# Weights decoded by shift, multiply-add and join, k transposed over the tile of P and sent by DMA, and another order of the program

## The chip, the cores and the metric

The kernel runs on one core of one Trainium2 chip. The metric is the device time of one execution in microseconds (us). The time of the kernel before is the median of three runs.

## What is computed

Gated linear attention followed by a feed-forward layer with ELU, all in float32. The shapes are 4 batches, 8 heads, 768 steps, head size 48; d_model 384, d_ff 2048, so 3072 tokens.

```python
for t in range(S):
    state = alpha[:, :, t, :, None] * state + einsum('bhd,bhe->bhde', k[:, :, t], v[:, :, t])
    y[:, :, t] = einsum('bhd,bhde->bhe', q[:, :, t], state)
x = y.transpose(0, 2, 1, 3).reshape(B * S, H * D)
h = x @ w_in
g = where(h > 0, h, exp(minimum(h, 0)) - 1)
out = g @ w_out
```

q, k, v and alpha are float32. The two weight matrices come in as float64: the kernel gets each value as two 32-bit words and makes a float32 of it on the chip.

## The kernel before

**Two phases that are interleaved.** The attention is cut into 24 windows of 128 steps (six for each batch). The feed-forward layer is cut into 12 blocks of 256 tokens (two windows each) and 8 slices j of d_ff. Weights and activations of the feed-forward layer are split into a high and a low part (type fp32r), and three products replace one: high by high, high by low, low by high.

**The order is written out by hand.** The function body defines small steps, each under a short name. Two strings list them: START for windows 0 to 11 and the first feed-forward blocks, with the decoding of the weights, and STEADY, which is repeated with a shift of two windows and one block a round. A step `KA.4` is step KA of window 4; `A.1.3` is step A of block 1, slice 3; in STEADY the numbers are relative to the round (`A.-2` is the slice two before the block's first one, `U.2` the window two after the round's first). Every engine takes its instructions in the order of the list, and each of its own steps waits for what it needs. DMAs are issued on SP's queue, in the list's order as well.

**The steps of a window i.**
- L (or LA and LB for windows 0 and 1) loads k, q and alpha of the window into one of 3 tiles `qka`; LV loads v into one of 4 tiles `vs`.
- SC: VectorE's running product of alpha, giving P (2 buffers). LN and EX (ScalarE): R = 1/P (2 buffers). KA, KB, KC: k divided by P with one correction step; `d["kt"]` is overwritten. KA and KB are on VectorE for a few windows and on GpSimd for the rest, KC is on VectorE. SQ: q times P into `st` (VectorE or GpSimd). PC: ScalarE copies P into R, for a sum that is checked.
- TP and KN (windows 0 to 5): TensorE transposes k into PSUM, ScalarE copies it to `kn`. TA and TB (windows 6 to 11) and T with a part number (from 12): VectorE transposes k into `kn` by 16 instructions for a window, each of 32 partitions x 128 elements (line 276, `blocks`).
- S: scores, k by q (lines 330 and 314), MK: the mask, on VectorE. U: the state's increments, transposed k by v (lines 376 and 358). UA, UB, UC: the states at the half and the end of the window. UP does part of it on TensorE for window 1.
- Y (for windows 0 to 3 with YL and Y3): the output, state and scores by v. XH, XL: its high and low part into `xt`; XP is XL's subtraction done on TensorE for windows 0 and 1. XD: two DMAs that put the fourth group of heads in its place.

**The steps of the weights.** F loads a weight slice f (768 KB) into `raw`; slices are decoded in pairs p of two slices. DA, DB, DC (lines 565, 571, 577) make the float32 bits from the two words on VectorE. WH (ScalarE) gives the high part, WL (ScalarE for slices 0 and 2, there with WP on TensorE; VectorE for 4; GpSimd for the others) the low part. Slices 2j belong to w_in, 2j + 1 to w_out. LC, CA and CB load a half slice again (`ck`, one buffer) and sum up two checks of its range on ScalarE; V and VP turn all sums into a flag that decides at the end whether a general, slower program must run.

**The steps of a block b and slice j.** A: 18 matmuls of 128x256 (line 639). RA and RB (ScalarE), RC (VectorE): ELU. GH (ScalarE) and GL (VectorE): its high and low part. O: 12 matmuls of 128x384 that add into the output (line 690). Z: two copies and two DMAs of the output.

**The start.** TensorE runs 16 matmuls on constants (X, line 126) until the first window's k is there.

## Time and profile before

| | |
|---|---|
| median of 3 runs | 503.76 us (503.52 to 504.37) |
| the profiled execution's own time | 503.54 us |
| its span, first to last instruction | 501.8 us |
| granted TensorE clock | 1.000 |
| PE (TensorE's matmuls) | 491.7 us busy, 98% of the span |
| PEld (TensorE's weight loads, beside the matmuls) | 474.4 us, 95% |
| DVE (VectorE) | 385.9 us, 77% |
| ACT (ScalarE) | 289.7 us, 58% |
| POOL (GpSimd) | 128.3 us, 26% |
| DMA | 61.13 MB in 22403 packets |

Busy shares are means over the whole span; the slices of the profile show them in 40 equal parts, as tenths. The chain of work follows the execution back from its last instruction, at each step to what released it. Matmuls overlap, so the pace of a group is read from one start to the next and not from the duration of one matmul. A time in square brackets is how long the engine had been idle, with what ended it. SPq is the queue on which SP issues DMAs.

### The profile page before, as it was taken

Reading aid. Unit: us, or ns where it says so; the run is one execution under the profiler, and the core shown is the slowest. Engines: PE = TensorE matmul, PEld = TensorE weight load, DVE = VectorE, ACT = ScalarE, POOL = GpSimd, SP = SyncE. Lnnn points to the kernel's source line nnn. Section 1 sums busy time; section 2 is a strip of 40 time slices with the busy share of each in tenths; the row PEclk is TensorE's granted clock in tenths of the full one; section 3 lists DMA queues with packets and bytes.
Section 4 is the critical chain, followed back from the end, with each engine's and each line's share of the span. In section 5 each row is a group of like instructions: output and inputs, shape, how many; then the busy total and the mean of one; then the engine's idle time right before and its main releaser. Section 6 shows DMA issues by size and latency. Waiting matters only on the chain.

```text
span 501.8 us, 13252 instructions
## 1 busy us (share of the span) xinstructions
PE 491.7 (98%) x5404; PEld 474.4 (95%) x5404; DVE 385.9 (77%) x807; ACT 289.7 (58%) x689; POOL 128.3 (26%) x109
## 2 busy tenths in 40 slices
PE   7999999999999999999999999999999999999996
PEld 3799999999999899999999999999999999999995
DVE  6989999989998579769969969769969878344321
ACT  3656786456460677746755756647755755454432
POOL 4125565443320302501501501501501500000000
PEclk9999999999999999999999999999999999999999
DMA  8999323213522145226245145235233321110001
GB/s 312 413 410 377 97 96 142 88 50 106 189 64 64 51 137 177 65 81 217 55 122 179 48 125 180 58 112 183 72 111 100 92 77 49 51 44 6 3 33 36
DMA packets 22403, 61.13 MB, mean 122 GB/s; under 512 B 2880, under 2 KB 9792, under 8 KB 22336
## 3 DMA queue, kind: packets, MB, share of 16 engines
q1 hardware_dynamic: 22048, 59.83, 36.3%
q8 instruction: 44, 0.72, 0.6%
q10 hardware_dynamic: 288, 0.39, 0.2%
q14 instruction: 23, 0.19, 0.1%
HBM read 53.53 MB, written 4.72 MB: 116 GB/s over the span
## 4 chain that ended last, share of the span: by engine, by line
PE 95%; DVE 2%; ACT 1%; issue 1%; ACTq 0%
PE h L639 40%; PE o L690 40%; PE y L442 4%; PE y L437 2%; PE q L314 2%; PE q L358 1%; PE u L376 1%; PE wp L126 1%; PE sc L330 1%; PE y L481 1%; PE tp L266 1%; DVE kn L276 0%; PE yl L437 0%; PE wd L612 0%; DVE st L342 0%
## 5 line engine op out<-in xcount | busy, mean ns | idle before, releaser
L639 PE MATMUL h<-xt,w 128*128 128x256 f32 x1728 | 215.3, 282 | 0.0
L639 PEld LDWEIGHTS h<-xt,w 128*128 128x128 f32 x1728 | 209.3, 188 | 2.3 <-issue 0.9
L690 PE MATMUL o<-w,gh 128*128 128x384 f32 x768 | 199.3, 341 | 0.8 <-ACT gh L663 0.8
L690 PEld LDWEIGHTS o<-w,gh 128*128 128x128 f32 x768 | 136.8, 188 | 1.7 <-ACT gh L663 1.0
L690 PE MATMUL o<-w,gl 128*128 128x384 f32 x384 | 130.0, 339 | 0.1
L663 ACT CAST gh<-h 128x512 fp32r<-128x512 f32 x96 | 56.0, 583 | 78.4 <-PE o L690 39.9
L676 DVE TENSOR_TENSOR gl<-h,gh 128x512 fp32r<-128x512 f32 x96 | 65.6, 687 | 35.6 <-ACT gh L663 34.4
L276 DVE STREAM_TRANSPOSE kn<-qka 32x128 f32<-32x128 f32 x288 | 87.1, 302 | 4.5
L647 ACT ACTIVATE r<-h 128x512 f32<-128x512 f32 x96 | 57.1, 596 | 47.7 <-PE h L639 39.7
L657 DVE SCALAR_TENSOR_TENSOR h<-r,h 128x512 f32<-128x512 f32 x96 | 64.6, 689 | 17.0 <-ACT r L652 16.2
L690 PEld LDWEIGHTS o<-w,gl 128*128 128x128 f32 x384 | 72.1, 188 | 0.4 <-DVE gl L676 0.4
L222 POOL TENSOR_TENSOR qka<-qka,R 128x512 f32<-128x512 f32 x19 | 26.2, 1378 | 163.9 <-DVE gl L676 116.4
L652 ACT ACTIVATE r<-r 128x512 f32<-128x512 f32 x96 | 59.4, 631 | 0.7
L252 POOL TENSOR_TENSOR st<-qka,P 64x512 f32<-64x512 f32 x36 | 42.8, 1190 | 21.7 <-DVE P L200 16.3
L342 DVE TENSOR_TENSOR st<-q,mask 64x256 f32<-64x256 f32 x72 | 30.4, 422 | 11.8 <-ACT vs L393 9.0
L200 DVE TENSOR_TENSOR_SCAN P<-qka,first 128x516 f32<-128x516 f32 x24 | 30.4, 1267 | 2.8 <-DMA qka<-in_qka_dram 2.3
L227 POOL TENSOR_TENSOR R<-P,R 128x512 f32<-128x512 f32 x20 | 24.2, 1211 | 27.2 <-DVE qka L222 25.8
L209 ACT ACTIVATE R<-P 128x512 f32<-128x512 f32 x24 | 15.2, 632 | 27.7 <-DVE P L200 27.7
L395 DVE TENSOR_TENSOR vs<-vs,q 48x192 f32<-48x192 f32 x30 | 10.5, 349 | 18.0 <-PE q L314 16.1
L495 ACT ACTIVATE y<-y 128x128 fp32r<-128x128 f32 x20 | 5.5, 276 | 29.7 <-PE y L442 26.4
L623 POOL TENSOR_TENSOR w<-spare,w 128x768 fp32r<-128x768 f32 x7 | 15.2, 2173 | 25.8 <-ACT w L603 25.8
L595 ACT ACTIVATE ck<-ck,lim 128x384 f32<-128x384 f32 x32 | 20.7, 646 | 0.1
(100 smaller groups left out, 421.6 us busy)
## 6 DMA issues: line engine op xcount, KB each, us to landing
qka<-in_qka_dram SPq DMA_DIRECT2D x22, 770.0 KB, 6.4
raw<-in_wgt_dram SPq DMA_DIRECT2D x16, 768.0 KB, 13.4
ck<-in_wgt_dram SPq DMA_DIRECT2D x32, 384.0 KB, 3.2
vs<-in_vv_dram SPq DMA_DIRECT2D x36, 192.0 KB, 4.3
out_dram<-ot SPq DMA_DIRECT2D x22, 192.0 KB, 1.9
vs<-in_vv_dram SPq DMA_DIRECT2D x6, 384.0 KB, 12.3
xt<-y SPq DMA_DIRECT2D x40, 48.0 KB, 2.3
qka<-in_qka_dram SPq DMA_DIRECT2D x2, 512.0 KB, 4.9
```

Source lines behind the costliest of these rows:

```text
L200: nc.vector.tensor_tensor_scan(out=P.rearrange("p n w -> p (n w)"), data0=t[:, 2 * NP * W:], data1=first.rearrange("p n w -> p (n w)"), in ...
L222: eng(KAV, i).tensor_tensor(out=d["kt"], in0=d["kt"], in1=d["R"], op=ALU.mult)
L252: eng(SQV, i).tensor_tensor(out=st[r, a], in0=d["q"][r], in1=pw(i)[r], op=ALU.mult)
L276: nc.vector.transpose(out=kn[32 * t:32 * t + 32, :, 32 * g:32 * g + 32], in_=d["kt"][32 * g:32 * g + 32, :, 32 * t:32 * t + 32])
L342: nc.vector.tensor_tensor(out=d["st"][r, a, :, c * C:(c + 1) * C], in0=d["s4"][a][o], in1=mask[o].unsqueeze(1).broadcast_to([64, NP, C]), ...
L639: nc.tensor.matmul(h[:, f, :], lhsT=t[:, wi, ws], rhs=x[:, c, xi, :], start=(f == 0 and k == 0), stop=(k == 8), skip_group_check=True)
L647: nc.scalar.activation(out=r, in_=d["h"], func=AF.Relu, scale=-1.0)
L652: nc.scalar.activation(out=d["r"], in_=d["r"], func=AF.Exp, scale=-1.0)
L657: nc.vector.scalar_tensor_tensor(out=d["h"], in0=d["r"], scalar=-1.0, in1=d["h"], op0=ALU.add, op1=ALU.max)
L663: nc.scalar.copy(out=gh, in_=d["h"])
L676: nc.vector.tensor_tensor(out=gl, in0=d["h"], in1=d["gh"].bitcast(F32), op=ALU.subtract)
L690: nc.tensor.matmul(o[:, 0:DM], lhsT=gt[:, f, ms], rhs=t[:, wi, f * DM:f * DM + DM], start=(j == 0 and f == 0 and k == 0), stop=(j == NJ - ...
```

## The change

**Decoding.** The raw bytes are loaded 5 bytes further into their tile, so that the bits of interest stand in aligned words. DA is a shift of one word, DB a multiply-add over the top byte of each value (type uint8) that writes a small integer into the other word, DC a shift of that word joined with DA's result. The range check becomes narrower: CB makes two passes where it made one, and V compares one more row.

**k for U.** T is now one transposition of 128 x 512 elements that writes into the tile R (which held 1/P and then PC's copy of P). TM is new: four DMAs on SP's queue that bring the pieces to a tile `kx`, 64 KB each in runs of 256 bytes. U reads its stationary operand from `kx` with a step of two elements. TA, TB and `blocks` are gone. TP and KN for windows 0 to 5 stay.

**Order.** START and STEADY are written anew. The first loads, for one, go from LA.0 LB.0 LA.1 LB.1 LV.0 F.2 F.0 L.2 LV.1 to LA.0 LA.1 LB.0 LV.1 LB.1 LV.0 L.2 F.2 F.0.

```diff
 START = """
-LA.0 LB.0 SC.0 LN.0 EX.0 LA.1 KA.0 KB.0 LB.1 SC.1 X.2 LV.0 LN.1 X.2 KC.0 F.2 SQ.0 EX.1 F.0 TP.0 KN.0 S.0 U.0
-SQ.1 UA.0 KA.1 KB.1 MK.0 L.2 KC.1 UC.0 YL.0 LV.1 TP.1 PC.0 Y3.0 Y.0 KN.1 DA.0 PC.1 LV.2 DB.0 L.3 F.4 S.1 SC.2
...
+X.2 LA.0 LA.1 LB.0 SC.0 LN.0 EX.0 LV.1 SQ.0 SC.1 LB.1 X.2 LV.0 KA.0 KB.0 KC.0 SQ.1 TP.0 UB.1 L.2 LN.1 F.2 EX.1 KN.0
+KA.1 S.0 U.0 PC.0 KB.1 MK.0 UA.0 F.0 L.3 KC.1 YL.0 UC.0 TP.1 S.1 KN.1 U.1 SC.2 MK.1 LN.2 DA.0 UB.0 DB.0 F.6 UP.1 Y3.0
+UC.1 UA.1 DC.0 LV.2 F.4 PC.1 YL.1 EX.2 Y3.1 SC.3 KA.2 Y.0 WH.0 Y.1 LN.3 XH.0 F.3 SQ.2 WP.0 EX.3 XH.1 WH.2 WP.2 KA.3
+XP.0 KB.2 WL.0 XP.1 KC.2 TP.2 KB.3 DA.2 S.2 KN.2 XL.0 KC.3 U.2 DB.2 SQ.3 XL.1 F.1 L.4 DC.2 LV.3 TP.3 KN.3 WH.6 DA.1
+A.0.0 UB.2 U.3 UA.2 WH.4 MK.2 UC.2 YL.2 PC.2 WL.4 RA.0.0 F.7 DB.1 RB.0.0 SC.4 DC.1 WL.2 S.3 LN.4 F.5 MK.3 UB.3 WL.6
+A.0.3 WH.3 EX.4 LV.4 DA.3 F.8 SQ.4 A.0.2 UA.3 RA.0.3 Y3.2 A.0.1 YL.3 RC.0.0 RB.0.3 Y.2 KA.4 F.11 DB.3 L.6 KB.4 Y3.3
...
 STEADY = """
-A.-3 Y.1 XH.1 Y.0 XH.0 A.-2 XL.1 RA.-3 O.-5 RA.-2 XL.0 LV.4 U.2 CA.-12 V.0 RB.-3 S.2 UA.2 MK.2.0 U.3 UB.2 S.3
...
+A.-3 CA.-12 Y.1 Y.0 S.2 RA.-3 RB.-3 XH.1 U.2 XH.0 O.-5 L.5 CB.-12 XL.1 RC.-3 UA.2 GH.-3 A.-1 RA.-1 XD.1 XL.0 UB.2
+LC.-11 UC.2 RB.-1 U.3 MK.2.0 S.3 MK.2.1 XD.0 SC.4 LN.4 CA.-11 A.-2 UA.3 EX.4 A.3 RA.-2 UB.3 O.-4 RC.-1 MK.3.0 V.0
+GL.-3 RB.-2 LV.4 RC.-2 KA.4 UC.3 CB.-11 SQ.4 KB.4 MK.3.1 RA.3 LC.-10 A.1 GH.-2 A.0 RA.1 RB.3 RB.1 CA.-10 SC.5 GL.-2
+A.2 GH.-1 RC.1 GL.-1 O.-3 O.-2 LN.5 RA.0 EX.5 L.6 CB.-10 KA.5 KC.4 KB.5 LC.-9 O.-1 RB.0 RC.3 RA.2 RC.0 A.4 PC.4 RB.2
+GH.0 LV.5 GH.1 SQ.5 CA.-9 GL.0 GL.1 RA.4 O.0 CB.-9 RC.2 ZV.4 GH.2 T.4 TM.4 O.1 GL.2 RB.4 KC.5 LC.-8 PC.5 O.2 RC.4
+GH.3 GH.4 GL.4 Z.-1 T.5 VP.0 GL.3 TM.5
...
-    def blocks(i, gs):
...
-        for g in gs:
-            for t in range(4):
-                nc.vector.transpose(out=kn[32 * t:32 * t + 32, :, 32 * g:32 * g + 32],
-                                    in_=d["kt"][32 * g:32 * g + 32, :, 32 * t:32 * t + 32])
...
+    def T(i):
+        d = win[i]
+        tk = d["tk"] = d["R"].rearrange("p n w -> p (n w)").rearrange("p (t b x c) -> p t b x c", t=4, b=2, c=2)
+        nc.vector.transpose(out=tk.rearrange("p t b x c -> p (t b) c x"),
+                            in_=d["kt"].rearrange("p n (j t) -> p t n j", t=4))
+
+    @tok
+    def TM(i):
+        d = win[i]
+        kn = d["kx"] = work.tile([128, 2, 2, 64, 2], F32, name="kn", tag="kn")
+        for g in range(4):
+            nc.sync.dma_start(out=kn[:, :, g // 2, g % 2 * 32:g % 2 * 32 + 32].rearrange("p b x c -> p b (x c)"),
+                              in_=d["tk"][32 * g:32 * g + 32].rearrange("p t b x c -> p (t b) (x c)"))
...
-                nc.tensor.matmul(d["u"][x][64 * a:64 * a + D, n, :], lhsT=d["kn"][r, n, a, 0:D],
+                nc.tensor.matmul(d["u"][x][64 * a:64 * a + D, n, :], lhsT=d["kx"][r, n // 2, a, 0:D, n % 2] if "kx" in d else d["kn"][r, n, a, 0:D],
...
-            raw[p] = wtile(p, [128, 2, WCH, 2], I32, "raw")
-        nc.sync.dma_start(out=raw[p][:, k].rearrange("p k two -> p (k two)"), in_=wgt[f].bitcast(I32))
+            raw[p] = wtile(p, [128, 2, 8 * WCH + 64], U8, "raw")
+        nc.sync.dma_start(out=raw[p][:, k, 5:5 + 8 * WCH], in_=wgt[f].bitcast(U8))
...
+    def parts(p):
+        t = raw[p][:, :, 8:8 + 8 * WCH]
+        words = t.bitcast(I32).rearrange("p k (c two) -> p k c two", two=2)
+        return words[:, :, :, 0], words[:, :, :, 1], t.rearrange("p k (c x) -> p k c x", x=8)[:, :, :, 4]
...
-        nc.vector.tensor_scalar(out=mi, in0=hi32, scalar1=3, scalar2=0x3FFFFFFF,
-                                op0=ALU.logical_shift_left, op1=ALU.bitwise_and)
+        nc.vector.tensor_single_scalar(out=wm[p].bitcast(I32), in_=parts(p)[0], scalar=5,
+                                       op=ALU.logical_shift_right)
...
-        nc.vector.scalar_tensor_tensor(out=mi, in0=lo32, scalar=29, in1=mi,
-                                       op0=ALU.logical_shift_right, op1=ALU.bitwise_or)
+        word, top = parts(p)[1:]
+        nc.vector.tensor_scalar(out=word, in0=top, scalar1=1.125, scalar2=-63.4375, op0=ALU.mult, op1=ALU.add)
...
-        nc.vector.scalar_tensor_tensor(out=mi, in0=hi32, scalar=-2 ** 30, in1=mi,
-                                       op0=ALU.bitwise_and, op1=ALU.bitwise_or)
+        mi = wm[p].bitcast(I32)
+        nc.vector.scalar_tensor_tensor(out=mi, in0=parts(p)[1], scalar=27, in1=mi,
+                                       op0=ALU.logical_shift_left, op1=ALU.bitwise_or)
...
-        t = ck.pop(f).bitcast(F32)[:, :, 1]
-        nc.scalar.activation(out=t, in_=t, func=AF.Relu, scale=-1.0, bias=lim, accum_out=chk_w[:, 1, f:f + 1])
+        t = ck.pop(f).bitcast(F32)
+        for k, (sign, bias) in enumerate(((1.0, lim[:, 1:2]), (-1.0, lim[:, 0:1]))):
+            nc.scalar.activation(out=t[:, :, k], in_=t[:, :, 1], func=AF.Relu, scale=sign, bias=bias,
+                                 accum_out=chk_w[:, k, f:f + 1])
```

## The prediction

> **What bounds the kernel now.** I read the page first: busy shares, slices, chain of work.

> ```profile
> PE 491.7 (98%) x5404; PEld 474.4 (95%) x5404; DVE 385.9 (77%) x807; ACT 289.7 (58%) x689; POOL 128.3 (26%) x109
> ...
> PE   7999999999999999999999999999999999999996
> ...
> DVE  6989999989998579769969969769969878344321
> ...
> DMA  8999323213522145226245145235233321110001
> ...
> PE 95%; DVE 2%; ACT 1%; issue 1%; ACTq 0%
> ```

> TensorE is busy from the first slice to the last, and 95% of the chain is its own work. VectorE is nearly full only in the first eight slices (100 us), the DMA engines in the first four. So an edit that frees VectorE after 100 us frees time that nobody waits for. Then the table of stretches (columns: stretch, length, then busy us of PE, PEld, DVE, ACT, POOL) and the list of waits, for how much TensorE time is idle at all:

> ```profile
> 169.20:497.20 328.00, 327.89 (x3436) 322.38 (x3436) 235.61 (x540) 193.56 (x480) 59.63 (x53) 1.00 0.30 93
> ```

> ```profile
> PE o L690 <- ACT gh L663: 0.8, 1, 0.8
> ...
> PE yl L437 <- ACT vs L393: 0.4, 1, 0.4
> ...
> PE y L481 <- ACT y L470: 0.4, 1, 0.4
> ...
> PE wd L500 <- ACT w L603: 0.3, 1, 0.3
> ```

> In the steady part TensorE idles 0.11 of 328 us; the four waits add up to 1.9 us. The rest of what could be won lies ahead of the first real matmul. The order in time there (start, length, what):

> ```profile
> 2.08 6.13 PE L126 MATMUL wp<-first 128*128 128x512 bf16 x16 [2.08 <-DVE first L120]
> ...
> 3.73 1.23 DVE L200 TENSOR_TENSOR_SCAN P<-qka,first 128x516 f32<-128x516 f32 x1 [0.83 <-DMA qka<-in_qka_dram]
> ...
> 6.41 0.69 DVE L222 TENSOR_TENSOR qka<-qka,R 128x512 f32<-128x512 f32 x1 [1.45 <-ACT R L214]
> ...
> 8.89 0.66 DVE L232 SCALAR_TENSOR_TENSOR qka<-R,qka 128x512 f32<-128x512 f32 x1
> ...
> 9.66 0.63 PE L266 MATMUL tp<-ident,qka 128*128 128x128 f32 x4 [1.45 <-issue]
> ...
> 13.31 0.95 DVE L565 TENSOR_SCALAR wm<-raw 128x1536 int32<-128x1536 int32 x1
> ...
> 29.37 4.54 PE L639 MATMUL h<-xt,w 128*128 128x256 f32 x36
> ```

> **The change, part by part.** Matmuls are the same in number and size, so the time moves only through TensorE's waits and the order's own costs. Prices of the operations (columns: form, count, busy us, mean ns, idle before):

> ```profile
> L276 DVE STREAM_TRANSPOSE kn<-qka 32x128 f32<-32x128 f32 x288 | 87.1, 302 | 4.5
> ...
> L595 ACT ACTIVATE ck<-ck,lim 128x384 f32<-128x384 f32 x32 | 20.7, 646 | 0.1
> ...
> L623 POOL TENSOR_TENSOR w<-spare,w 128x768 fp32r<-128x768 f32 x7 | 15.2, 2173 | 25.8 <-ACT w L603 25.8
> L209 ACT ACTIVATE R<-P 128x512 f32<-128x512 f32 x24 | 15.2, 632 | 27.7 <-DVE P L200 27.7
> ...
> L496 ACT ACTIVATE xt<-y 128x384 fp32r<-128x384 f32 x24 | 11.6, 485 | 5.8 <-PE y L437 4.5 <-PE h L639 1.3
> ...
> L577 DVE SCALAR_TENSOR_TENSOR spare<-raw,spare 128x1536 int32<-128x1536 int32 x4 | 7.4, 1858 | 0.0
> ...
> L571 DVE SCALAR_TENSOR_TENSOR spare<-raw,spare 128x1536 int32<-128x1536 int32 x4 | 7.0, 1755 | 0.1
> ...
> L603 ACT CAST w<-spare 128x768 fp32r<-128x768 f32 x8 | 6.7, 838 | 0.7 <-DVE spare L577 0.7
> ...
> L426 DVE SCALAR_TENSOR_TENSOR vs<-u,P 128x192 f32<-128x192 f32 x2 | 0.7, 353 | 0.0
> ```

> *Decode.* DA stays a one-input step (0.96 us, the 13.31 row). DC keeps its form (1.75 to 1.86). DB turns from a two-input step (1.755) into a one-input step over bytes that stand 8 bytes apart, written 8 bytes apart. No row has a one-byte input. Bounds: 0.95, DA's form, and 1.76, the step that it replaces. I take 0.96: the 13.31 row reads words 8 bytes apart and takes little more than half of L571's time, and DB is nearest to it. That is 0.8 us less on VectorE for each of 8 pairs.

> [...]

> *k over P.* Sixteen transpositions of 302 ns a window (4.8 us) become one of 128x512. Bounds 0.69 us (the pace of L222) and 1.21 us (four of L276's); I take 1.0, so 18 windows free 68 us of VectorE. It lies beside other work, price on the path 0. T writes into R, so it waits for PC and KC, and R comes free for LN two windows on only when TM's copies have landed; both have half a period or more. TM's price is on SP's queue; the nearest copies are those of XD:

> ```profile
> L529 SPq DMA_DIRECT2D xt<-y x12: 583/612/640, 182.3 to 259.5; - x12
> ...
> DMA to landing us min/median/max: 2.2/2.3/3.2
> ```

> Four issues of 0.61 make 2.4 us of SP, and 2.3 to 3.2 us to landing. In STEADY the tighter one is TM.5, behind T.5, LC.-8 and the two Z copies. Counting from the end of A.4: CB's second pass and GH.2 to GH.4 put GL.4 near 7, T.5 near 8, the last copy lands at 13 to 14. U.3 follows O.0, O.1, O.2, A.5, Y, Y, S.2, U.2, O.3 and A.7 at about 16. Two us are left: price 0.

> *U reads kx at a step of two words.* No row has a stepped TensorE operand. Lower bound 0 (nothing can make it cheaper), upper bound the block of U doubled, 18 x 0.51 = 9.2 us. I take 0, after L571's read at that step.

> *F writes 5 bytes further.* Same rows of 6,144 bytes; 0, and at most one load's time more, which would act as a late decode does (below).

> *CB twice.* 32 x (0.65 and its accumulator read of about 0.2) = 27 us on ScalarE, 59% busy in the steady stretch; it rises to about 66%. LC, XD.0 behind it on SP, GH and RA wait up to 0.85 us longer; XD.0 lands near 7 us after Y.0 and its reader A.3 starts 8.7 us after it. Price 0, cover 1.7 us.

> *The order.* Ahead of KA.0 VectorE idles 1.45 us. After, SC.1 (1.23) stands in that hole and not between KB.0 and KC.0, so KC.0 ends near 8.55 instead of 9.55, and TP.0 starts at 8.65 instead of 9.66; the warm-up ends at 8.2 and hides no more. **-1.0 us** at this point. But the decode gives it back. In the queue LV.1 and L.2 now stand ahead of F.2 and F.0. The nine loads up to F.0 are exactly the nine that before end with LV.1:

> ```profile
> L187 SPq DMA_DIRECT2D vs<-in_vv_dram x1: 722/722/722, 4.7 to 4.7; - x1
> ...
> DMA to landing us min/median/max: 11.2/11.2/11.2
> ```

> So F.0 lands at 4.65 + 11.2 = 15.85, and DA.0 starts there, 2.5 us later than now. From it: DA, DB, UC.1, DC and SC.3 on VectorE, 0.96 + 0.96 + 0.35 + 1.75 + 1.25 = 5.3, to 21.2; LN.3, XH.0, EX.3, XH.1 and WH.2 on ScalarE, two of 0.63, two of 0.49, one of 0.84 and three accumulator reads, 3.7, to 24.9; then the end of WP.2, XP, TP.2, S.2, U.2 and TP.3 on TensorE, from these pieces of the chain (start, length, what):

> ```profile
> 27.30 1.13 PE u L376 x29
> 28.50 0.94 PE sc L330 x31
> ...
> 33.91 0.44 PE tp L266 x4
> ```

> With 1.5 for WP.2 and XP that is 4.7, so A.0.0 starts at 29.6 against 29.37, with TP.3 (0.44) done, which before comes later. The start comes out at **-0.2 us**: the gain at TP.0 turns into a wait at WP.2 of about 2 us.

> From there VectorE works without a hole up to DC.5: five each of DA, DB and DC (18.4), three scans (3.7), 8 products (5.6), the small steps of windows 1 to 4 and the first RC and GL (11.1), some 38.8 with 1.7 of gaps: 15.85 + 40.5 = 56.4. WH.9, CA.0, RB.1.1, GH.0.2 and WH.5 follow on ScalarE (3.7), WL.5 on GpSimd (2.2), 62.3. O.0.2, which reads it, is due after A.0.0, eight A and two O of 2.1 in all (the rows below), 10.7 us of small matmuls of windows 2 to 4 (2.3 a Y, 1.1 to 1.2 an S or U, about 0.5 a YL or TP) and three changes of 0.18: 29.6 + 21.2 + 10.7 + 0.5 = 62.0. It misses by the 0.2 that the sum counts, no more.

> Each change from small fp32 matmuls to the large ones costs time, as the chain shows in the steady part:

> ```profile
> 213.82 2.13 PE h L639 x18
> 215.96 2.02 PE y L442 x64
> 217.97 2.31 PE h L639 x18
> ...
> 222.41 0.51 PE q L358 x32
> ...
> 254.16 2.02 PE y L442 x64
> ```

> 18 matmuls take 2.13 in the run and 2.31 after Y: 0.18. (From Y to Y a round is 38.2 us.) Written out, TensorE's order has 31 such changes before and 28 after: **-0.55 us**. And one wait goes, the longest of the list:

> ```profile
> 168.39 0.62 PE L690 MATMUL o<-w,gh 128*128 128x384 f32 x2 [0.77 <-ACT gh L663]
> ```

> The chain ahead of it is VectorE's masks, eight transpositions and a scan; with T and SQ elsewhere it has 4 us to spare. **-0.77**, and nothing is late next there that I find. The steady part and the tail: 0.

> Sum: -0.2 - 0.55 - 0.77 = -1.5, and +0.2 for WL.5: -1.3. The profiled execution took 503.54 (span 501.8); it becomes 502.2. It lies 0.22 below the median of the runs, so I forecast **502.4**.

> **Rivals.**
> *DB takes the 1.76 us of the step that it replaces (slower).* Five DBs stand ahead of WL.5, whose slack is nil: 5 x 0.8 = 4.0 us; 502.4 + 4.0 = 506.4. It decides from 0.96 + 1.3/5 = 1.22 us a DB. For it: no row with bytes; against it: the 13.31 row's pace. A late F would act the same way.
> *No change.* The 1.3 us that the sum gains go into waits at WL.5, YL.2 and YL.3, whose inputs VectorE, ScalarE and GpSimd hand over within half a microsecond of the due time: 503.7. For it: VectorE full up to 100 us; against it: three changes of operand kind fewer cost nothing to anyone.
> *The copies of TM land late,* behind LC, L or Z: U.3 waits. Beyond the 2 us of cover each us costs 7 us over the 7 steady rounds with a U.3; one us gives 509.4. For it: pieces of 256 bytes, which no row has; against it: XD's 2.3 us.
> *Stepped reads slow TensorE:* half of the bound, 4.6, gives 507.0; for and against as above.

> **How the numbers follow.** Forecast 0.48 (its own range 501.2 to 503.2), DB 0.15, no change 0.23, TM 0.08, stepped reads 0.06. The low end is all four waits and both start terms gone, 503.76 - 1.9 - 1.0 - 0.55 = 500.3; the high end takes in DB's case: 500.3 to 507.0, which leaves out about 0.17. A measurement of this kernel tells some 0.2% (1.0 us) from no change; faster by more 0.44 (of the forecast's 0.48), within it 0.27, slower 0.29.

> **What would show it.** Right: TP.0 near 8.6, DA.0 near 15.9, an idle of about 2 us at WP.2's L500, A.0.0 near 29.6, no PE wait near 168, the steady round still 38.2 us, DB near 0.96. Wrong: DB at 1.7 with PE waiting on POOL's w around 62; U's block above 0.51; PE waiting on a DMA into kn; landings of raw beyond 1.9 us a load.

## The result, and the profile after

The changed kernel takes 510.08 us (median of 4 runs, 509.63 to 512.54); the kernel before takes 503.75 in the same session. The ratio is 1.0134 (95% interval 1.010 to 1.017): 6.3 us slower, where I forecast 1.3 us faster and a range of 500.3 to 507.0. The profiled execution took 509.63, its span 507.9. The mean granted TensorE clock was 1.000 in the profiled run before; in the four runs after it was 0.982, 0.977, 0.980 and 0.983. Medians below take in every run, but a ratio leaves out runs more than 1.5% above the fastest of the same kernel (three of run 5, one of run 7).

That last number is the finding. The page of the changed kernel shows it in its slices (PE busy, the clock granted in tenths, DMA):

```profile
PE   6999999999999999999999999999999999999996
...
PEclk9589999999999999999999999999999999999999
DMA  8995733332542345345245345245345232100001
```

TensorE is as "busy" as before from the second slice on, but in slice 2 and part of slice 3 at half its clock. The table of stretches has it finer (stretch, length, busy us of PE, PEld, DVE, ACT, POOL, then the granted clock, DMA share, GB/s); first the changed kernel, then the kernel before:

```profile
7.90:11.30 3.40, 1.39 (x12) 0.69 (x12) 3.33 (x5) 0.06 (x1) 1.30 (x1) 1.00 1.03 414
11.30:28.30 17.00, 15.87 (x212) 13.70 (x210) 10.04 (x13) 5.92 (x15) 2.73 (x2) 0.50 1.01 411
28.40:400.00 371.60, 370.57 (x4262) 361.83 (x4261) 253.92 (x427) 248.54 (x608) 125.59 (x91) 1.00 0.43 136
```

```profile
7.20:10.60 3.40, 1.96 (x21) 1.09 (x21) 3.13 (x5) 1.56 (x4) 0.00 (x0) 1.00 1.04 402
10.60:28.30 17.70, 16.67 (x318) 13.44 (x315) 16.75 (x19) 10.81 (x29) 2.74 (x2) 1.00 1.02 413
```

For 17 us TensorE is busy 15.9 us, yet it issues 212 matmuls where the kernel before issues 318 in much the same time. VectorE and ScalarE, much of whose work waits for it, fall from 16.8 and 10.8 us of work to 10.0 and 5.9. A busy share alone would not have shown that. In order of time (start, length, what, idle before; first TensorE, then VectorE, then GpSimd):

```profile
10.57 0.63 PE L267 MATMUL tp<-ident,qka 128*128 128x128 f32 x4 [2.01 <-issue]
11.13 1.87 PE L324 MATMUL sc<-st,qka 48*64 48x64 f32 x32
...
37.66 2.36 PE L636 MATMUL h<-xt,w 128*128 128x256 f32 x18
```

```profile
7.47 0.69 DVE L223 TENSOR_TENSOR qka<-qka,R 128x512 f32<-128x512 f32 x1 [1.35 <-DMA qka<-in_qka_dram]
8.20 1.55 DVE L228 TENSOR_TENSOR R<-P,R 128x512 f32<-128x512 f32 x1
...
19.23 0.69 DVE L341 TENSOR_TENSOR st<-sc,mask 128x512 f32<-128x512 f32 x1 [2.09 <-PE sc L324]
19.84 0.95 DVE L560 TENSOR_SCALAR wm<-raw 128x1536 int32<-128x1536 int32 x1
```

```profile
7.52 1.67 POOL L250 TENSOR_TENSOR st<-qka,P 128x512 f32<-128x512 f32 x1 [3.89 <-DMA qka<-in_qka_dram]
```

The same S.0 took 1.15 us before (10.21 to 11.29); now 1.87. TP.0 starts 0.9 us later than before, A.0.0 8.3 us later (TP.3, 0.4, is done by then). From A.0.0 to the last copy of the output (497.13 before, 503.87 after) the changed kernel is 1.5 us *faster*. So the whole loss lies ahead of A.0.0, and nearly all of it between TP.0 and A.0.0.

TP.0 is late because KA.0 waits for LB.0, now third in the queue behind LA.1. From its issue at 1.75 it needed 5.63 us (by the chain of work) and landed at 7.38; before, second in the queue, it landed at 5.14. Then KB.0 takes 1.55 us beside SQ.0 on GpSimd, which waited for the same load (0.69 before). Of the list of waits (us in total, times, longest) the last is new in the steady part:

```profile
PE tp L267 <- issue: 2.0, 1, 2.0
PE yl L431 <- ACT vs L387: 1.1, 2, 0.9
PE h L636 <- DMA xt<-y: 0.9, 1, 0.9
```

### The profile page after: what moved, and what is told of

It reads as the page before. It is cut to its first block, busy times and chain, and to the rows that moved or that the text cites. A ratio compares the mean times of both kernels' runs of the same rounds, so it can differ in the third digit from the quotient of the medians.

```text
span 507.9 us, 13216 instructions
## 1 busy us (share of the span) xinstructions
PE 497.6 (98%) x5404; PEld 480.9 (95%) x5404; DVE 314.7 (62%) x538; ACT 312.6 (62%) x753; POOL 135.7 (27%) x109
## 4 chain that ended last, share of the span: by engine, by line
PE 95%; DMA 2%; ACT 1%; issue 1%; POOL 0%; SPq 0%; DVE 0%; ACTq 0%; DVEq 0%; POOLq 0%
PE o L687 40%; PE h L636 40%; PE y L436 4%; PE y L431 2%; PE q L308 2%; PE u L370 2%; PE sc L324 2%; PE q L352 1%; DMA qka<-in_qka_dram 1%; DMA xt<-y 1%; PE y L475 1%; PE tp L267 1%; PE yl L431 1%; PE wd L609 1%; POOL st L250 0%
## 5 line engine op out<-in xcount | busy, mean ns | idle before, releaser
L673 DVE TENSOR_TENSOR gl<-h,gh 128x512 fp32r<-128x512 f32 x96 | 64.5, 683 | 67.9 <-ACT gh L660 67.7
L654 DVE SCALAR_TENSOR_TENSOR h<-r,h 128x512 f32<-128x512 f32 x96 | 66.1, 690 | 63.9 <-ACT r L649 63.6
L660 ACT CAST gh<-h 128x512 fp32r<-128x512 f32 x96 | 54.5, 579 | 21.6 <-PE o L687 14.7
L253 POOL TENSOR_TENSOR st<-qka,P 64x512 f32<-64x512 f32 x36 | 46.0, 1277 | 4.0 <-issue 2.6
L591 ACT ACTIVATE ck<-ck,lim 128x384 f32<-128x384 f32 x64 | 41.2, 644 | 1.0
L228 POOL TENSOR_TENSOR R<-P,R 128x512 f32<-128x512 f32 x20 | 28.1, 1404 | 23.5 <-DVE qka L223 16.3
L336 DVE TENSOR_TENSOR st<-q,mask 64x256 f32<-64x256 f32 x72 | 30.3, 420 | 2.6 <-PE q L308 1.2
L585 ACT ACTIVATE ck<-ck 128x384 f32<-128x384 f32 x32 | 17.8, 557 | 7.7 <-DMA ck<-in_wgt_dram 7.5
L512 DVE TENSOR_TENSOR y<-y,y 128x128 fp32r<-128x128 f32 x20 | 5.8, 289 | 26.6 <-ACT xt L490 23.8
L274 DVE STREAM_TRANSPOSE R<-qka 128x512 f32<-128x512 f32 x18 | 19.7, 1095 | 2.1 <-ACT R L237 2.1
L210 ACT ACTIVATE R<-P 128x512 f32<-128x512 f32 x24 | 15.2, 635 | 9.2 <-DVE P L201 7.6
```

Source lines behind the costliest of these rows:

```text
L228: eng(KBV, i).tensor_tensor(out=d["R"], in0=pw(i), in1=d["R"], op=ALU.mult)
L253: eng(SQV, i).tensor_tensor(out=st[r, a], in0=d["q"][r], in1=pw(i)[r], op=ALU.mult)
L336: nc.vector.tensor_tensor(out=d["st"][r, a, :, c * C:(c + 1) * C], in0=d["s4"][a][o], in1=mask[o].unsqueeze(1).broadcast_to([64, NP, C]), ...
L591: nc.scalar.activation(out=t[:, :, k], in_=t[:, :, 1], func=AF.Relu, scale=sign, bias=bias, accum_out=chk_w[:, k, f:f + 1])
L654: nc.vector.scalar_tensor_tensor(out=d["h"], in0=d["r"], scalar=-1.0, in1=d["h"], op0=ALU.add, op1=ALU.max)
L660: nc.scalar.copy(out=gh, in_=d["h"])
```

## The experiments

Theory: LB.0's place leaves TensorE idle for 2.0 us, the clock falls for 17 us, and that is most of the loss. Rivals: the delay itself (VectorE and the weights are late); or the new operations. Ratios are to the kernel before on the same chip.

**1. LB.0 second.** One DMA moves; on every other queue the order is that of the changed kernel.

```diff
-X.2 LA.0 LA.1 LB.0 SC.0 LN.0 EX.0
+X.2 LA.0 LB.0 LA.1 SC.0 LN.0 EX.0
```

> The changed kernel with LB.0 issued second, ahead of LA.1, instead of third; no other instruction moves. Theory A (the clock): LB.0 lands near 5.1 us instead of 7.38, KA.0 starts near 6 and TP.0 near 8.7 instead of 10.57, TensorE's idle ahead of TP.0 falls from 2.0 us to under 0.6, the granted clock stays at 1.0 to the end (mean above 0.995 instead of 0.982), the small matmuls of windows 0 and 1 are back at 1.1 to 1.2 us a group, A.0.0 starts at 30 to 31.5 and the time is 502.5 to 504.5. Theory B (the delay alone): only the 2.2 us of the late landing come back, 507.5 to 508. Theory C (the copies of TM, the stepped reads or the second pass of CB cost the time): 509 to 510, with the clock up or not.

502.59 us (501.45 to 505.34, 12 runs), ratio 0.9973 (0.9957 to 0.9990): the 6.3 us of loss became a gain of 1.7 us by the medians, 1.4 by the ratio. Stretches and time line:

```profile
11.30:28.30 17.00, 15.46 (x282) 12.65 (x280) 15.22 (x20) 8.79 (x24) 2.43 (x2) 1.00 1.02 416
```

```profile
5.98 1.68 DVE L201 TENSOR_TENSOR_SCAN P<-qka,first 128x516 f32<-128x516 f32 x1 [1.10 <-DMA qka<-in_qka_dram]
7.59 0.66 DVE L223 TENSOR_TENSOR qka<-qka,R 128x512 f32<-128x512 f32 x1
...
15.98 0.95 DVE L560 TENSOR_SCALAR wm<-raw 128x1536 int32<-128x1536 int32 x1
```

```profile
9.80 0.63 PE L267 MATMUL tp<-ident,qka 128*128 128x128 f32 x4 [1.35 <-issue]
...
30.48 1.79 PE L636 MATMUL h<-xt,w 128*128 128x256 f32 x13
```

In the profiled run the clock stays up and A.0.0 comes 7.2 us earlier, of which TP.0's own gain is 0.8. (Two of the twelve runs, 505.2 and 505.3, have a mean clock of 0.993, under the expected 0.995; they have no trace.) Theory C falls: every new operation is still there. The expected 8.7 for TP.0 was a miss: SC.1 stands ahead of KA.0 on VectorE, waits for LA.1 and takes 1.68 us beside SQ.0 on GpSimd (1.22 before), so KA.0 starts at 7.59. I had put SC.1 into VectorE's hole; it overfills it.

**2. LB.0 still third, but more warm-up.**

```diff
-LB.1 X.2 LV.0 KA.0 KB.0
+LB.1 X.12 LV.0 KA.0 KB.0
```

> The changed kernel with ten more warm-up matmuls (X.12 for the second X.2), which keep TensorE busy from 8.5 to about 10.6 us; LB.0 still lands at 7.4 and TP.0 still starts at 10.6. Theory A (the clock): no idle ahead of TP.0, granted clock 1.0 (mean above 0.995), A.0.0 at 31.5 to 33 and the time 503.5 to 505.5, that is up to 2 us above the kernel with LB.0 second, which is the price of the delay without the clock. Theory B (the delay alone): 509 to 510 as before the edit. Theory C: 509 to 510.

505.66 us (503.85 to 509.81, 12 runs), ratio 1.0031 (1.0008 to 1.0054). Ten matmuls that compute nothing take 4.4 us off the 510.08, with the data as late as before (LB.0 landed at 7.69, TP.0 started at 10.89). At the full clock they ended at 9.82, so 1.07 us of idle were left, where none was expected, and the clock fell for one window only, after a later gap of 1.17 us:

```profile
6.10:19.70 13.60, 10.98 (x172) 7.63 (x171) 10.27 (x14) 4.82 (x14) 2.87 (x2) 1.00 1.01 401
19.70:23.10 3.40, 3.40 (x46) 2.95 (x48) 3.40 (x4) 2.72 (x7) 0.48 (x1) 0.50 1.01 417
```

```profile
PE h L636 <- ACT ck L585: 1.6, 1, 1.6
```

The second fence is a wait in the steady part, at 190 us: LC's load was issued at 184.58 behind XD.1 on SP's queue, CA on ScalarE waited 1.75 us for it, and ScalarE's other steps stand behind CA. It is the same stretch of the round as the 0.9 us at 348 us.

**3. The kernel before, with LB.0 third.**

```diff
-LA.0 LB.0 SC.0 LN.0 EX.0 LA.1 KA.0
+LA.0 LA.1 LB.0 SC.0 LN.0 EX.0 KA.0
```

> The kernel before with LA.1 issued ahead of LB.0, and nothing else changed. Theory A (the clock): LB.0 lands near 7.4 instead of 5.14, KA.0 starts 1 us later, TP.0 at 10.6 to 11, TensorE idles 2.3 to 2.7 us ahead of it, the clock falls to half for five windows of about 3.4 us (mean 0.98) and the time is 508 to 511. Theory B (the delay alone): 504.8 to 506, clock 1.0.

509.52 us (508.74 to 511.0), ratio 1.0115 (1.0097 to 1.0134). The swap alone breaks the old kernel in the same way; TP.0's delay of 2.2 us alone would have ended near 506. Time line and stretches:

```profile
11.82 0.63 PE L266 MATMUL tp<-ident,qka 128*128 128x128 f32 x4 [4.01 <-DVE qka L232]
```

```profile
13.20:20.00 6.80, 6.54 (x84) 5.36 (x81) 5.21 (x7) 2.42 (x7) 1.18 (x1) 0.50 0.98 364
```

TP.0 came later than I expected (11.82, not 10.6 to 11): KB.0 takes 1.55 here too, and SC.1 stands between KB.0 and KC.0. In the profiled run two windows ran at half clock; the mean clocks of the runs are 0.987 to 0.991.

**4. The kernel before, with 12 warm-up matmuls for 16.** No data is later; TensorE only idles longer.

```diff
-SC.1 X.2 LV.0 LN.1 X.2 KC.0
+SC.1 LV.0 LN.1 KC.0
```

> The kernel before with 12 warm-up matmuls in place of 16, and nothing else changed: TP.0 stays at 9.66, its inputs are no later, only TensorE idles about 2.4 us ahead of it instead of 1.45. Theory A (idle ahead of TP.0 sets the clock): the clock falls to half near 10.6 us for three to five windows (mean 0.98 to 0.99), time 507 to 510. Theory B (the delay alone): 503.5 to 504, since no work is later.

507.84 us (506.3 to 508.11), ratio 1.0062 (1.0044 to 1.0081). This is the cleanest test: TP.0 starts where it did, and the loss comes from idle time alone.

```profile
9.65 1.08 PE L266 MATMUL tp<-ident,qka 128*128 128x128 f32 x4 [2.98 <-issue]
10.67 1.97 PE L330 MATMUL sc<-st,qka 48*64 48x64 f32 x32
```

```profile
9.20:19.50 10.30, 9.58 (x118) 8.11 (x120) 7.24 (x10) 4.16 (x11) 1.18 (x1) 0.50 1.02 417
```

A.0.0 starts at 33.39 where it was 29.37 before: 4.0 us for 10.24 us at half clock. The kernel before may have little to spare even as it stands: of its 84 runs beside these experiments five, on two chips, took 507.0 to 507.3 with a mean clock of 0.991. No trace of them was kept, so whether their start failed in this way isn't known.

**5. XD.0 ahead of LC.-11 in the steady order** (with LB.0 second, as in all that follow).

```diff
-XL.0 UB.2 LC.-11 UC.2 RB.-1 U.3 MK.2.0 S.3 MK.2.1 XD.0 SC.4
+XL.0 XD.0 UB.2 LC.-11 UC.2 RB.-1 U.3 MK.2.0 S.3 MK.2.1 SC.4
```

> The changed kernel with LB.0 issued second and, in the steady order, XD.0 put straight behind XL.0, ahead of LC.-11 on SP's queue. Theory A (the 0.9 us in which TensorE waited at 348 us for the DMA into xt, and the spread between runs, come from XD.0 standing behind LC.-11, which waits for ScalarE's CB.-12): no wait of TensorE on a DMA into xt, the spread of the runs narrower than the 3.9 us of the kernel without this edit, median 501.3 to 502.3. Rival (the wait is rare and the spread comes from the granted clock): median 502.3 to 503, spread as before. Second rival: LC.-11 is now late and ScalarE's CA.-11 holds up RA and GH: above 503.

502.91 us (500.63 to 509.81, 12 runs), ratio 0.9949 (0.9924 to 0.9974): not to be told from run 1, whose interval it overlaps. No wait for xt in its profile, but run 1's had none of note either, so what XD's place is worth stays open. The spread got wider, not narrower: three runs took 508.3 to 509.8 with a mean clock of 0.980 to 0.983. Run 7 below shows what such a start looks like, there with the old decode.

**6. SC.1 behind KC.0**, so that KA.0 doesn't wait for LA.1.

```diff
-LV.1 SQ.0 SC.1 LB.1 X.2 LV.0 KA.0 KB.0 KC.0 SQ.1 TP.0
+LV.1 SQ.0 LB.1 X.2 LV.0 KA.0 KB.0 KC.0 SC.1 SQ.1 TP.0
```

> The kernel with LB.0 second and XD.0 early, and SC.1 moved behind KC.0 on VectorE. Theory A (SC.1 held KA.0 back: it started at 5.98 behind LA.1 and took 1.68 us beside SQ.0 on GpSimd, so KA.0 started at 7.59 and TP.0 at 9.80): KA.0 starts near 6.4, TP.0 near 8.6, TensorE idles under 0.4 us ahead of it, A.0.0 0.5 to 1 us earlier than 30.5, the time 0.5 to 1.2 us under the kernel without this edit. Rival (the window-1 chain ends last): TP.1 or YL.1 waits longer by what TP.0 gained, A.0.0 at 30.3 to 31, time the same within 0.5 us.

507.19 us (505.23 to 508.85), ratio 1.0047 (1.0026 to 1.0069): slower, and neither expectation foresaw it. TP.0 came at 8.63, as the prediction had wanted it, with 0.73 us of idle. But LN.1, now waiting for SC.1, and EX.1 stand ahead of KN.0 on ScalarE:

```profile
8.63 0.63 PE L267 MATMUL tp<-ident,qka 128*128 128x128 f32 x4 [0.73 <-issue]
...
11.61 1.21 PE L370 MATMUL u<-vs,kn 128*64 128x48 f32 x29 [1.28 <-ACT kn L289]
```

```profile
13.40:27.00 13.60, 12.73 (x152) 10.88 (x154) 8.67 (x11) 5.13 (x14) 1.55 (x1) 0.50 1.02 415
```

The idle time moved from ahead of TP.0 to among the small matmuls and cost four windows. All eight runs have a mean clock of 0.983 to 0.993.

**7. The old decode in the repaired order of run 1.**

```diff
-        nc.vector.tensor_scalar(out=word, in0=top, scalar1=1.125, scalar2=-63.4375, op0=ALU.mult, op1=ALU.add)
+        nc.vector.scalar_tensor_tensor(out=mi, in0=lo32, scalar=29, in1=mi,
+                                       op0=ALU.logical_shift_right, op1=ALU.bitwise_or)
...
```

> The changed kernel with LB.0 second, and the loads and decode of the weights (F, DA, DB, DC) as in the kernel before: DB is the two-input step of about 1.76 us again instead of 0.95. Theory A (VectorE sets the end of the first 60 us, as the prediction's first rival priced it: five steps of 0.8 us): A.0.0 0.8 to 1.6 us later, O.0.2 4 us later, time 506 to 507. Rival (the decode has slack in this order, and the new one gains nothing): 502.3 to 503.3, the wait at most 1 us.

509.02 us (506.01 to 513.62), ratio 1.0085 (1.0052 to 1.0118), but with mean clocks from 0.979 to 0.997, so two effects are mixed; run 11 repeats it. The profiled run, 513.62 and the longest of the six, shows how a start fails even with LB.0 second: LA.1 landed 6.0 us after its issue (4.2 in run 1), and SC.1 held KA.0 back.

```profile
7.75 1.23 DVE L201 TENSOR_TENSOR_SCAN P<-qka,first 128x516 f32<-128x516 f32 x1 [2.86 <-DMA qka<-in_qka_dram]
```

**8. All new operations in the old order.**

```diff
-T.4.1 ... T.4.2 ... T.4.3 ... T.5.2 ... T.5.1 ... T.5.0 ... T.4.0 T.5.3 LC.-8
+T.4 TM.4 T.5 TM.5 LC.-8
```

> All new operations (decode, one transposition and four DMAs a window, CB twice, the stepped reads of kx) in the order of the kernel before; each window's T and TM stand where the last of its four transpositions stood. Theory A (the loss is the order's alone, and the operations cost and gain nothing on TensorE's path): clock 0.996 or more, time 503 to 505, within 0.2% of the kernel before. Rival 1 (the operations cost time: copies late, ScalarE's second pass): 505.5 or more, with TensorE waiting for a DMA into kn or xt in the steady part. Rival 2 (the operations alone gain what the repaired kernel gains): 502 to 502.8.

505.52 us (504.38 to 507.72, 12 runs), ratio 1.0022 (1.0003 to 1.0041), clock 0.997 to 1.000. The operations cost about 1.2 us in the old order, just outside theory A. The profile shows new waits, 4.5 us in all, more than was lost; most are on VectorE's steps and not on the DMAs that rival 1 named, and what was gained against them isn't traced:

```profile
PE h L635 <- DVE st L335: 3.1, 2, 1.7
...
PE h L635 <- DVE P L200: 0.7, 1, 0.7
PE h L635 <- DMA xt<-y: 0.7, 1, 0.7
```

The start is as good as before (TP.0 at 9.55, A.0.0 at 29.26). So the operations alone are not the loss, and placed like this they are no gain either; another place for T and TM was not tried.

**9. Six more warm-up matmuls on run 5's kernel.**

```diff
-LB.1 X.2 LV.0 KA.0
+LB.1 X.8 LV.0 KA.0
```

> The kernel with LB.0 second and XD.0 early, and six more warm-up matmuls (X.8 for the second X.2; about 1.3 us at full clock), so that TensorE's idle ahead of TP.0 is under 0.5 us where it was 1.65. Theory A (the idle ahead of TP.0 still decides about the clock in those runs in which LA.1 lands late, and this makes the runs with a mean clock near 0.98): no run under a mean clock of 0.99, A.0.0 unchanged at 30.3, median 500.6 to 502.5 and no run above 505. Rival (the runs at 508 to 510 have another cause): one run in four still at 508 or more with a clock near 0.98. Second rival (the added matmuls delay TP.0): A.0.0 up to 0.5 us later.

502.2 us (500.53 to 502.66, 6 runs), ratio 0.9932 (0.9905 to 0.9959), and no run near 508. Four runs at 502.1 to 502.7 have a mean clock of 0.996, the two at 500.5 and 500.7 have 1.000. So no start failed as in run 5. But TP.0 came at 9.79 with 1.03 us of idle, not under 0.5. A run of the first kind was profiled; there YL.1's idle falls into one window, the next runs at half clock, and A.0.0 comes at 31.98 where it was 30.33 in run 5:

```profile
18.53 0.68 PE L431 MATMUL yl<-st,vs 48*64 48x64 f32 x15 [1.17 <-ACT vs L387]
```

```profile
15.90:19.30 3.40, 2.23 (x40) 1.81 (x40) 3.40 (x5) 1.16 (x4) 0.00 (x0) 1.00 1.01 409
19.30:22.70 3.40, 3.40 (x50) 2.93 (x50) 2.74 (x4) 1.91 (x5) 1.18 (x1) 0.50 1.01 416
```

**10. A shorter chain to TP.0**: SC.1 behind KC.0, KN.0 ahead of LN.1 and EX.1, three more warm-up matmuls.

```diff
-SQ.0 SC.1 LB.1 X.2 LV.0 KA.0 KB.0 KC.0 SQ.1 TP.0 UB.1 L.2 LN.1 F.2 EX.1 KN.0
+SQ.0 LB.1 X.5 LV.0 KA.0 KB.0 KC.0 SC.1 TP.0 SQ.1 UB.1 L.2 KN.0 LN.1 F.2 EX.1
```

> The kernel with LB.0 second and XD.0 early; SC.1 behind KC.0 on VectorE, KN.0 ahead of LN.1 and EX.1 on ScalarE, SQ.1 behind TP.0, and three more warm-up matmuls. TP.0 then depends on the loads LA.0 and LB.0 alone. Theory A: TP.0 near 8.6, U.0 near 10.3 with no wait for ScalarE's KN.0, no idle above 0.5 us up to U.0; TP.1 waits for KC.1 at 13 to 14 (1 to 1.5 us idle), the clock stays up, A.0.0 at 29.8 to 30.6, time 500.5 to 502.5. Rival (the idle has only moved to TP.1, among small matmuls, as it moved to U.0 in the kernel with SC.1 later): the clock falls to half at 13 to 17 us for two to five windows, mean 0.98 to 0.99, time 504 to 508.

506.77 us (502.75 to 508.93, 12 runs), ratio 1.0035 (1.0014 to 1.0055). The rival held: the idle went to YL.0, TP.1 and YL.1, and the mean clock is 0.984 to 0.993 in all runs but one (0.996). That one, the fastest, is the run that was profiled; it has one window at half clock, 19.03 to 22.45.

```profile
8.68 0.63 PE L267 MATMUL tp<-ident,qka 128*128 128x128 f32 x4 [0.71 <-issue]
12.59 0.61 PE L431 MATMUL yl<-st,vs 64*64 64x64 f32 x12 [1.01 <-DVE st L341]
13.97 0.66 PE L267 MATMUL tp<-ident,qka 128*128 128x128 f32 x4 [0.77 <-DVE qka L233]
19.12 1.17 PE L431 MATMUL yl<-st,vs 48*64 48x64 f32 x16 [1.36 <-ACT vs L387]
```

**11. The old decode in run 9's kernel** (the edit of run 7, which also puts the loads F back as they were).

> The kernel with LB.0 second, XD.0 early and six more warm-up matmuls, with the loads and decode of the weights of the kernel before (DB two-input, 1.76 us for 0.95). It repeats the test of the old decode at an equal clock. Theory A (VectorE sets the end of the first 60 us in this order; five to eight steps of 0.8 us): 3 to 5 us above the kernel with the new decode, clock above 0.99 in both. Rival (the decode has slack): within 1 us of it.

508.62 us (505.83 to 512.98, 12 runs), ratio 1.0077 (1.0046 to 1.0108). Eight runs have a mean clock of 0.980 to 0.993. The four at 0.997 to 0.998 took 505.83 to 506.27; run 9 at 0.996 took 502.14 to 502.66. Against those and against run 9's two at 1.000 (500.6) the old decode costs 3.8 to 5.5 us in this order (DB at 1.75 for 0.95); a mean of 0.997 doesn't tell whether one window ran at half clock, since the fall after the last matmul counts in it too (in the changed kernel at 506.23, 2.4 us after that matmul's end). In the profiled run (511.06) LA.1 landed 6.1 us after its issue, as in run 7, and TensorE idled 2.78 us ahead of TP.0; in the profiles of runs 1, 5, 9 and 12 it took 4.1 to 4.5. Why the starts failed more often with this edit isn't known: the first instruction of the decode starts long after, but F.2, whose place in the tile the edit moves, is issued at 4.15, before LA.1 lands.

**12. Run 9 with both gaps filled**: four more matmuls ahead of TP.0 and five ahead of YL.1.

```diff
-LB.1 X.8 LV.0 KA.0
+LB.1 X.12 LV.0 KA.0
-F.6 UP.1 Y3.0
+F.6 UP.1 X.5 Y3.0
```

> The kernel of bridge2 with four more warm-up matmuls ahead of TP.0 (X.12) and five between UP.1 and YL.1, where TensorE idled 1.17 us among small matmuls and, in the profiled run, the clock fell for one window (19.33 to 22.74 us). Theory A (each window with over a microsecond of idle among small matmuls can cost a half-clock window, worth 1.5 to 1.9 us): no half clock between 6 and 490 us in any run, mean clock 0.999 or more, A.0.0 at 30.2 to 30.6, median 500.4 to 501.2, about 1.5 us under bridge2's 502.2. Rival (dummy matmuls of 128x512 do not count, or the fall has another cause): most runs stay at 0.996 and 502.2 to 502.7. Second rival: the added matmuls delay YL.1, median above 502.7.

502.26 us (500.83 to 503.94, 8 runs), ratio 0.9958 (0.9941 to 0.9975). In the profiled run (500.83) no window from 4.90 us to the end runs at half clock, as theory A said:

```profile
4.90:499.00 494.10, 489.17 (x5413) 475.07 (x5411) 313.42 (x529) 311.87 (x752) 132.59 (x96) 1.00 0.41 131
```

But the median isn't 1.5 us under run 9's, and the intervals overlap. Two of the longer runs (502.62 at 0.999, 503.06 at 0.998) have no window at half clock by their means, so something else makes them long, and the gain of this step is not shown. One difference of that size is seen: from the last output copy's start to the end of the span it takes 4.0 us here and 5.9 in run 1, after all matmuls are done. Runs 1, 5, 9 and 12 all lie under the kernel before, by 0.3 to 0.7%.

## Why the prediction was wrong, and where it was right

- **TP.0 at 8.65 (the term of -1.0): wrong, 10.57.** Two steps failed. I took SC.1's time off VectorE's path, which leaves KA.0 at its old start of 6.41, and had no term for LB.0's new place: in the queue before, LB.0 landed second at 5.14 and a third load of half its size at 5.97; as third, LB.0 took until 7.38, and KA.0 started at 7.47. And I priced KB.0 at the pace it had alone, though SQ.0 became its neighbour on GpSimd: 1.55. Run 6 got TP.0 to 8.63 and lost all the same.
- **The clock: not in the prediction at all.** It is the term that decided. I took the clock of 1.000 before as a constant and the start as 1.0 us to be won; that TensorE's idle ahead of TP.0, 1.45 us before, could grow and cost more than its length was put at nothing. Of the 6.3 us, run 2 recovers 4.4 by the medians (5.2 by the ratios) with the data as late as before. Between TP.0 and A.0.0 it is 27.1 us after, 20.7 in run 1: 6.4 for five windows, 1.3 each. Run 4 gives 4.0 for three, run 9 against run 1 gives 1.5 for one.
- **DA.0 at 15.85, A.0.0 at 29.6: wrong in the changed kernel (19.84, 37.66), nearly right once the clock is up.** In run 1 DA.0 is at 15.98 and A.0.0 at 30.48. F.0's landing was sized well (15.36), but the path behind it was not the one that counts: VectorE was at MK.1 from 15.37 and DA.0 followed it without a wait for the load, TensorE didn't wait at WP.2 at all, and what it waited for was YL.1's input (1.17), with UC.1 behind DB.0 on VectorE. So that these two times nearly agree is in part luck. (The rows from which I took 4.7 us for the last piece add up to 4.45.)
- **After A.0.0: right in sign.** I had -0.55, -0.77 and +0.2 (-1.1), with 0.44 for TP.3 done earlier: -1.5. Measured -1.5, with 0.9 lost to a wait for xt. The wait near 168 is gone; none at WL.5. So about a microsecond more was gained than my terms hold; it is not traced, and that the two sums agree is in part luck.
- **DB 0.96: right** (0.955, min/median/max over 8 in the first row below), and so that rival fell, but its price agrees with run 11: 4.0 forecast, 3.8 to 5.5 there, with F's loads changed as well. Writing words that stand 8 bytes apart cost DB nothing that shows: 955 ns for 1536 elements is 0.62 ns an element, and DA, which writes its words side by side, has medians of 957 and 1023 ns in the same profile.
- **T 1.0: right within a tenth; U's stepped reads 0: right** (205 ns a matmul before):

```profile
L567 DVE TENSOR_SCALAR raw<-raw x8: 949/955/1310, 20.7 to 99.2; 128x1536 int32<-128x1536 uint8 x8
L274 DVE STREAM_TRANSPOSE R<-qka x18: 1079/1095/1115, 103.5 to 412.4; 128x512 f32<-128x512 f32 x18
L352 PE MATMUL q<-vs,kn x528: 202/207/247, 112.6 to 422.4; 64*48 64x48 f32 x176
```

- **TM's copies: right**, 2.2 us to landing and nobody waits for kn. **CB twice: its cover of 1.7 us for XD.0 was too thin.** It ran out once in the changed kernel (0.9 us) and, through LC, once in run 2 (1.6); run 8 shows such waits too. The step took one landing (2.3 us) for all; XD's now take 2.1 to 5.9, median 3.7.

## What to carry to other kernels

In these runs a gap on TensorE had two prices: its own length, and the half clock that could follow, 1.3 to 1.7 us for every 3.4 us window. Before moving a load or a step ahead of the first real matmul, add up TensorE's idle time in any 3.4 us there, and look at the clock's row after the change before anything else. Dummy matmuls in a gap that was there anyway went with a clock that held past it: in run 2 (full up to 19.7 us) they won back 4.4 us, and in run 9 TP.0 came no later for them (9.79, 9.80 in run 1).

## What the runs showed of the hardware

| run | window, us | idle in it | beside it | next window |
|---|---|---|---|---|
| before | 7.18 to 10.59 | 1.45 | warm-up, TP, S | full |
| 5 | 6.76 to 10.17 | 1.65 | warm-up, TP | full |
| 3 | 6.38 to 9.80, then to 13.21 | 1.98, then 2.02 | warm-up alone, then TP, S | full, half |
| changed | 7.88 to 11.30 | 2.01 | 0.7 us of warm-up, TP, S | half |
| 4 | 5.83 to 9.24 | 2.56 | warm-up | half |
| 6 | 9.95 to 13.37 | 1.65 | small matmuls alone | half |
| 2 | 16.30 to 19.71 | 1.17 | small matmuls alone | half |
| 9 | 15.91 to 19.33 | 1.17 | small matmuls alone | half |
| 5 | 17.00 to 20.42 | 1.17 | small matmuls alone | full |
| 10 | 12.20 to 15.62, then to 19.03 | 1.16, then 1.28 | small matmuls alone | full, half |
| 1 | 14.48 to 17.89, then to 21.31 | 0.52, then 0.65 | small matmuls | full, full |

Runs 9, 2, 5 and 1 have the same gap of 1.17 us ahead of YL.1. In run 1 the edge of a window cuts it in two and the clock stays up; in runs 9 and 2 it lies whole in one window and the clock falls; in run 5 it lies whole in one window too, and the clock stays up:

```profile
18.40 0.73 PE L431 MATMUL yl<-st,vs 48*64 48x64 f32 x16 [1.17 <-ACT vs L387]
```

```profile
17.00:20.41 3.41, 2.24 (x49) 1.77 (x48) 3.41 (x4) 2.40 (x7) 0.00 (x0) 1.00 1.02 407
```

So the idle time in a window doesn't decide alone. In run 5 YL.1 and what follows it share the window with the gap, in run 9 it is mostly what stands ahead of it; whether that is the reason was not tested. What can be said: in the first 42 us of the 14 profiles no window at full clock with less than 1.17 us of idle was followed by one at half clock; from 1.17 to 2.0 us both came out, and all five with more (2.01, 2.02, 2.56 in the table, 2.04 in run 7, 2.75 in run 11) were. Where the edges of the grid fall differs from one profile to the next (5.83 in run 4, 6.38 in run 3, 7.18 before, 7.88 in the changed kernel, with the warm-up's start at 2.08 or 2.09 in all four); that this is why one program pays in some runs and not in others (run 9: a mean of 0.996 in four, 1.000 in two) is my estimate. How long small matmuls keep the clock down once it has fallen, one window in run 9 and five in the changed kernel, stays open; in the changed kernel it stayed down behind two windows in which TensorE shows no idle at all (11.30 to 14.71 and 18.12 to 21.54).
